# V loads on another queue, whole-batch DMA transposes and a reordered first tile in an attention-plus-MLP kernel

## The chip, the cores and the metric

The kernel runs on one core of one Trainium2 chip. The metric is device time in microseconds (us) for one execution, from the first instruction to the last. A core has several engines that run their own instruction streams side by side: TensorE (PE, with its weight loads listed as PEld), VectorE (DVE), ScalarE (ACT), GpSimd (POOL) and SyncE (SP). SP computes nothing here; it issues DMAs. Sixteen DMA engines move the data, whoever issues the DMA.

## The reference

Eight batches of eight heads, 576 positions of 64 elements, go through causal attention with a window of 64 positions. The heads of a position are laid side by side, which gives x with 4608 rows of 512. A gated MLP with 2048 hidden units follows.

```
scores = scale * np.matmul(q, k.transpose(0, 1, 3, 2))
mask = (rel >= 0) & (rel < window)
scores = np.where(mask, scores, -1000000000.0)
attn = np.exp(scores - max); attn = attn / sum(attn)
x = (attn @ v).transpose(0, 2, 1, 3).reshape(B * S, H * D)
h = x @ w_in
g = h * np.clip(h + 3.0, 0.0, 6.0) / 6.0
out = g @ w_out
```

## The kernel before, in words

**Two kinds of work on one TensorE stream.** The MLP is cut into nine tiles of 512 rows (T = 0 to 8). A tile has a first half, `s1` (16 column blocks of the hidden layer, four matmuls each, into a PSUM bank chosen by `s1_bank`; ACT and DVE make the gate `gT`, lines 538 and 539), and a second half, `s2` (16 steps of four matmuls, line 568, into the banks `o` and `acc`; a finished 128-row block is copied by ACT and stored, line 577). Both halves are generators; after each `yield` other work can be put between. That other work is the attention of a later batch: a tile's 512 rows are less than a batch's 576, so batch b has to be ready a little before tile b starts. There is no scheduler: the order of each engine's instructions is the order in which the Python program emits them (`tc.manual_schedule`), and each engine and each DMA queue runs its own in that order, waiting on semaphores where data is not there.

**What attention of a batch needs.** Heads are taken in four pairs g. Q and K arrive as float32, POOL casts them to bf16 (`qn_all`, `kn_all`), and they must be transposed to Q^T and K^T (`QT`, `KT`). For batches 0 and 1 the PE does that (`main_t`, called by `T_` and `TT`; `rest_t`, called by `RR`, for the last 64 positions). From batch 2 on DMA transposes do it, issued by SP: batch 2 with one for each pair and operand (`transpose_pairs_by_dma`, eight, line 280), the later ones with one for each operand (`transpose_by_dma`, lines 271 to 275). Then `scores` makes the score blocks of a pair in two halves u (line 354), ACT takes the exponential (line 362), `masked` multiplies by the mask on DVE (line 372), `pv` multiplies by V and divides by the sums (`N_`), and the result is transposed into `xT`, the MLP's input: on the PE with an ACT copy (`xt_pe`, `X_`, lines 417 and 422) for batches 0 to 3, by a DMA transpose on SP (`xt_dma`, line 477) for batches 4 to 7.

**Where these calls stand.** For batch 1 they are written out by hand between the steps of tile 0's second half: each `go()` is one step of `s2`. `rest_s`, `rest_n`, `rest_x` finish the last 64 positions of batch 0 there. From tile 1 on `stage_` runs a tile, and `pieces` says after which step of `s1` (p1) or `s2` (p2) a call of the next batch stands. Batch 2 goes through tile 1, batch 3 through tile 2, and so on. Batch 3 has a row of its own in `pieces`, with its first scores after step 13 of tile 2's `s1` and its `X_` calls in tile 2's `s2`. In tiles 1 and 2 the last two x^T transposes of the tile's own batch are put between the first matmuls of the tile.

**The queues.** The POOL queue takes, in this order, the first weights `w_in`, Q and K of batch 1 (heads 0 to 3), the rest of the weights, the tails of batches 0 and 1, and at last tile 0's four held output blocks (line 845). Between these stand POOL's casts. SP's queue takes Q, K, V of batch 0; V of batch 1, held back by `after` until the third block of `w_out` has landed; the 15 loads of batch 2 (Q, K, V, five each); its eight transposes; and then for each tile T the 15 loads of batch T + 2, the tile's output stores, the x^T transposes of batch T + 1, and the two transposes of batch T + 2. A transpose in the queue waits for POOL's casts, a store for ACT's copy, and all behind it wait too:

```
            p2.setdefault(6 if T < 3 else 12, []).append(lambda bt=nxt: bt.transpose_by_dma())
```

so in tiles 1 and 2 of the kernel before, the two whole-operand transposes stand after step 6 of `s2`, behind one store.

Of the kernel before, what the change touches and what calls it, by code (L numbers as in the profile page):

```python
# [24 lines left out]
def kernel(  # L25
# [53 lines left out]
    def load_v(b, vst, h0, h1):  # L79
        out = []  # L80
        for h in range(h0, h1):
            out.append(nc.sync.dma_start(
                out=vst[:, 0 : KB - 1, h, :],
                in_=v[b, h, 0:SM, :].rearrange("(k p) d -> p k d", p=P),
            ))
        return out

    def load_blocks(t, src, b, kbs, tail=0):
        out = []
        for kb in kbs:  # L90
            s0 = kb * P
            ss = min(P, S - s0)
            p0 = tail if ss < P else 0
            out.append(nc.sync.dma_start(  # L94
                out=t[p0 : p0 + ss, kb, :, :],
                in_=src[b, :, s0 : s0 + ss, :].rearrange("h s d -> s h d"),
            ))
        return out
# [22 lines left out]
    def load_v_by_head(b):  # L121
        vst = stage.tile([P, KB, H, D], F32, name="vst", tag="vst")
        ins = load_blocks(vst, v, b, (KB - 1,), SR) + load_v(b, vst, 0, H)
        return vst, ins

    def load_for_dma(b):
        sts, ins = [], []
        for n, src in (("qst", q), ("kst", k), ("vst", v)):
            t = stage.tile([P, KB, H, D], F32, name=n, tag=n)
            ins += load_blocks(t, src, b, range(KB), SR if src is v else 0)  # L130
            sts.append(t)
        return tuple(sts), ins
# [108 lines left out]
    class Batch:  # L241
# [28 lines left out]
        def transpose_by_dma(self):  # L270
            for n, T in ((qn_all, self.QT), (kn_all, self.KT)):
                nc.sync.dma_start_transpose(
                    out=T[:].rearrange("d g (k s) -> d (g k) s", s=P),
                    in_=n[:].rearrange("p g k h d -> p (g k h d)"),
                )

        def transpose_pairs_by_dma(self):
            for g in range(NG):
                for n, T in ((qn_all, self.QT), (kn_all, self.KT)):
                    nc.sync.dma_start_transpose(  # L280
                        out=T[:, g, :].rearrange("d (k s) -> d k s", s=P),
                        in_=n[:, g, :, :, :].rearrange("p k h d -> p (k h d)"),
                    )
# [210 lines left out]
    def s1_bank(fc, T):  # L494
        if T == 0:
            if fc in (6, 7):
                return (ps_o, ps_acc)[fc - 6].tile([P, 512], F32, name=("o", "acc")[fc - 6])[:]
            if fc in (8, 9, 12, 13):
                return ps_st.tile([P, 2, 512], F32, name=f"st{fc % 2}")[:, 0, :]
            return h_bank()[:]  # L500
        if T > 1 and fc < 2:
            return ps_st.tile([P, 2, 512], F32, name=f"st{fc}")[:, 0, :]
# [152 lines left out]
    w_in.append(load_w_in(1536, 2048, 0, NG))  # L655
    w_out = [load_w_out(0, 4)]
# [52 lines left out]
    ld.rest()  # L709
# [14 lines left out]
    bt.cast_qk(st, 1, 0, 4, pcopy)  # L724
    w_out += [load_w_out(4 * i, 4 * i + 4) for i in (1, 2)]
    rst0, rvst0 = load_rest_of_first()
    w_out.append(load_w_out(12, 16))
    vst1, insv = load_v_by_head(1)
    for x in insv:
        after(x, w_out[2], "the weights go first")  # L730
    bt.cast_rest(st, pcopy)
    cast_pairs(bt, st, 4, 4)
    bt0.cast_rest((None, None, rst0), pcopy)
# [4 lines left out]
    run(m)  # L738

    pcopy(out=bt0.V[SR:P, KB - 1, :, 0:D], in_=rvst0[SR:P, :, :])  # L740
    bt.cast_v_end(vst1, pcopy)
    for g in range(NG):
        bt.cast_v(vst1, 2 * g, 2 * g + 2, pcopy)
    st2, _ = load_for_dma(2)

    def st_tr(u):
        t = ps_st.tile([P, 2, 1024], BF16, name=f"st{u}")
        return iter((t[:, 0, :], t[:, 1, :]))

# [13 lines left out]
    S1_(0, 0, 0)  # L763
    S1_(1, 0, 1)
    go(2)
    RR(bt, st_tr(0))
    go()
    S1_(0, 1, 1)
    go()
    S1_(1, 1, 0)  # L770
    TT(bt, 2, st_tr(1))
    go(2)
    TT(bt, 3, st_tr(0))
    go()
    S1_(2, 0, 1)
    go()
    S1_(2, 1, 0)
    go()
    S1_(3, 0, 1)
    go()  # L780
    S1_(3, 1, 0)
    go()
    RR(bt0, st_tr(1))
    go()
    rest_s(bt0, 0)
    go()
    rest_n(bt0, 1)
    go()
    N_(bt, 0, st_pair(0))
    go()  # L790
    N_(bt, 1, oa)
    rest_x(bt0, 0)
    go()
    two = st_tr(1)
    X_(bt, 0, two)
    X_(bt, 1, two)
# [23 lines left out]
    def pieces(bt):  # L820
# [4 lines left out]
        if bt.b == 2:  # L825
            return p1, {
                1: [f(SS, 0)], 2: [f(SS, 1)], 4: [f(N_, 0), f(SS, 2)], 6: [f(X_, 0)], 7: [f(N_, 1), f(SS, 3)],
                9: [f(X_, 1)], 11: [f(N_, 2)], 13: [f(N_, 3)],
            }
        if bt.b == 3:  # L830
            return {13: [f(SS, 0)]}, {
                0: [f(SS, 1)], 3: [f(N_, 0), f(SS, 2)], 5: [f(X_, 0)], 6: [f(N_, 1), f(SS, 3)],
                8: [f(X_, 1)], 9: [f(N_, 2)], 11: [f(X_, 2)], 12: [f(N_, 3)], 14: [f(X_, 3)],
            }
# [8 lines left out]
    bt2.cast_for_dma(st2, (0, 1))  # L843
    for u0, osb in held:
        nc.gpsimd.dma_start(out=out[u0 : u0 + P, :], in_=osb[:])
    bt2.cast_for_dma(st2, (2,))
    bt2.transpose_pairs_by_dma()
    nxt, pend = bt2, None
    for T in range(1, NTB):
# [3 lines left out]
        if b < B:  # L853
# [5 lines left out]
            p2.setdefault(6 if T < 3 else 12, []).append(lambda bt=nxt: bt.transpose_by_dma())  # L859
# [31 lines left out]
```

## Time and profile before

| | us |
|---|---|
| median of 5 runs (lowest to highest) | 315.57 (314.49 to 317.58) |
| the profiled execution | 315.3 |
| its span, first to last instruction | 313.5 |
| PE busy in the span | 299.6 |
| DVE, ACT, POOL busy | 174.3, 177.6, 93.3 |
| start of tile 1, 2, 3, 4 on the PE | 58.1, 92.3, 127.4, 158.9 |
| bytes moved by DMA | 52.80 MB |

The 1.8 us between the span and the execution's time lie outside the instructions. The page lists busy time for each engine, then the span in 40 slices of 7.8 us with the busy share in tenths; its DMA row is the mean busy share of the 16 DMA engines. "a <- b" in a list of waits means that a waited for b. In the chain of waits each row is a start, a duration and what ran; a DMA's row runs from its issue to its landing. In the timeline of SP a row is the time in which SP issued, not the time in which the data moved. "L94" is line 94 of the kernel; `SPq` is SP's queue.

### The profile page before, as it was taken

What the parts mean: (1) busy time and instruction counts of PE and PEld (TensorE: products, weight loads), DVE (VectorE), ACT (ScalarE), POOL (GpSimd) and SP (SyncE); (2) the same over time, 40 slices, a digit from 0 to 9 for tenths busy, and PEclk for the clock granted to TensorE, in tenths of its full rate; (3) what the DMA queues carried; (4) which work ended last, traced back from release to release, by engine and by line L of the source; (5) the groups of instructions that cost most, each with busy time, mean ns of one, the idle gap of its engine ahead of it and who ended that gap; (6) DMA issues with size and microseconds to landing.
All of it is one profiled execution on the core that took longest, in us unless ns stands there. A gap on an engine that the chain in (4) does not pass through costs nothing.

```text
span 313.5 us, 5579 instructions
## 1 busy us (share of the span) xinstructions
PE 299.6 (96%) x2125; PEld 147.8 (47%) x2162; DVE 174.3 (56%) x334; ACT 177.6 (57%) x264; POOL 93.3 (30%) x137
## 2 busy tenths in 40 slices
PE   8898989899999899999999999999999999999995
PEld 3454435544654355445544554455445544444442
DVE  4558545485635765477437753785378627306700
ACT  3857744487627754687158715881588147317611
POOL 5786626363035143305610660155000000000000
PEclk9999999999999999999999999999999999999999
DMA  7999999999799999999999999999900730010011
GB/s 245 201 206 255 242 193 191 213 190 234 165 207 188 268 217 182 205 252 204 216 223 223 203 216 235 216 201 192 246 10 2 127 94 0 33 69 33 0 69 67
DMA packets 147579, 52.80 MB, mean 168 GB/s; under 512 B 136384, under 2 KB 142528, under 8 KB 147552
## 3 DMA queue, kind: packets, MB, share of 16 engines
q1 hardware_dynamic: 141920, 44.18, 69.1%
q0 software_dynamic: 5360, 8.00, 12.9%
q8 instruction: 17, 0.28, 0.4%
q10 hardware_dynamic: 272, 0.26, 0.2%
q14 instruction: 10, 0.08, 0.1%
HBM read 36.70 MB, written 9.44 MB: 147 GB/s over the span
## 4 chain that ended last, share of the span: by engine, by line
PE 73%; DMA 14%; SPq 4%; POOL 2%; ACT 2%; DVE 2%; issue 1%; POOLq 0%
PE o L568 17%; PE acc L568 16%; PE h L531 15%; PE acc L531 5%; PE o L531 5%; PE st L531 5%; DMA wout<-in_moe_w_out_dram 4%; PE st L354 3%; DMA qst<-in_q_dram 3%; DMA kst<-in_k_dram 3%; DMA vst<-in_v_dram 3%; SPq L94 2%; PE h L384 2%; DMA KT<-kn 1%; PE h L389 1%
## 5 line engine op out<-in xcount | busy, mean ns | idle before, releaser
L531 PEld LDWEIGHTS <-win 128*128 128x128 bf16 x576 | 55.1, 98 | 66.0 <-issue 1.7
L568 PEld LDWEIGHTS <-gT 128*128 128x128 bf16 x576 | 52.5, 98 | 57.9 <-issue 1.4
L568 PE MATMUL o<-wout,gT 128*128 128x512 bf16 x261 | 63.8, 380 | 1.5 <-DMA wout<-in_moe_w_out_dram 0.8
L531 PE MATMUL h<-xT,win 128*128 128x512 bf16 x259 | 62.8, 379 | 0.3
L568 PE MATMUL acc<-wout,gT 128*128 128x512 bf16 x261 | 62.3, 379 | 0.6
L362 ACT ACTIVATE pT<-st 128x768 bf16<-128x768 f32 x64 | 48.7, 808 | 14.6 <-PE st L354 14.4
L539 DVE SCALAR_TENSOR_TENSOR gT<-t,st 128x512 bf16<-128x512 bf16 (+1 forms) x26 | 20.7, 809 | 56.7 <-ACT t L538 56.6
L538 ACT ACTIVATE t<-h,half 128x512 bf16<-128x512 f32 x66 | 44.7, 690 | 8.6 <-PE h L531 8.2
L539 DVE SCALAR_TENSOR_TENSOR gT<-t,h 128x512 bf16<-128x512 bf16 x66 | 44.6, 685 | 8.9 <-ACT t L538 8.8
L372 DVE TENSOR_TENSOR pT<-pT,mask 128x1536 bf16<-128x1536 bf16 x28 | 28.2, 1011 | 22.5 <-ACT pT L362 22.5
L258 POOL CAST qn<-qst 128x512 bf16<-128x512 f32 x24 | 16.4, 719 | 71.1 <-DMA qst<-in_q_dram 66.9
L574 ACT COPY osb<-acc 128x512 f32<-128x512 f32 x17 | 10.0, 586 | 42.5 <-PE acc L568 42.5
L531 PE MATMUL st<-xT,win 128*128 128x512 bf16 x125 | 30.4, 379 | 0.7 <-DVE gT L539 0.3
L574 ACT COPY osb<-o 128x512 f32<-128x512 f32 x17 | 10.0, 588 | 29.9 <-PE o L568 29.9
L406 DVE TENSOR_TENSOR opg<-h,rec 128x320 bf16<-128x320 f32 x50 | 24.6, 492 | 1.7
L531 PE MATMUL o<-xT,win 128*128 128x512 bf16 x89 | 23.4, 379 | 0.5 <-DVE gT L539 0.3
L538 ACT ACTIVATE t<-st,half 128x512 bf16<-128x512 f32 (+1 forms) x26 | 20.1, 785 | 6.4 <-PE st L531 6.1
L531 PE MATMUL acc<-xT,win 128*128 128x512 bf16 x91 | 23.6, 379 | 0.1
L248 POOL CAST V<-vst 128x512 bf16<-128x512 f32 (+1 forms) x14 | 16.5, 1179 | 16.6 <-DMA vst<-in_v_dram 13.7
L384 PEld LDWEIGHTS <-pT 128*128 128x128 bf16 x256 | 17.5, 97 | 7.7 <-PE h L417 0.5
L258 POOL CAST kn<-kst 128x512 bf16<-128x512 f32 x24 | 14.4, 639 | 18.7 <-DMA kst<-in_k_dram 15.0
L354 PE MATMUL st<-QT,KT 64*128 64x192 bf16 (+2 forms) x312 | 17.5, 230 | 1.7 <-DMA KT<-kn 0.9
(111 smaller groups left out, 282.3 us busy)
## 6 DMA issues: line engine op xcount, KB each, us to landing
out_dram<-osb SPq DMA_DIRECT2D x32, 256.0 KB, 2.5
qst<-in_q_dram SPq DMA_DIRECT2D x28, 256.0 KB, 4.8
kst<-in_k_dram SPq DMA_DIRECT2D x27, 256.0 KB, 5.5
vst<-in_v_dram SPq DMA_DIRECT2D x24, 256.0 KB, 5.4
vst<-in_v_dram SPq DMA_DIRECT2D x23, 128.0 KB, 4.1
win<-in_moe_w_in_dram POOLq DMA_DIRECT2D x4, 512.0 KB, 7.4
wout<-in_moe_w_out_dram POOLq DMA_DIRECT2D x4, 512.0 KB, 13.3
qst<-in_q_dram POOLq DMA_DIRECT2D x2, 512.0 KB, 11.7
```

The source lines that it names most:

```text
L248: copy(out=self.V[:, 0 : KB - 1, h0:h1, 0:D], in_=vst[:, 0 : KB - 1, h0:h1, :])
L258: pcopy(out=n[:, g, 0 : KB - 1, :, :].rearrange("p k h d -> p k (h d)"), in_=s[:, 0 : KB - 1, 2 * g : 2 * g + 2, :].rearrange("p k h d -> ...
L354: nc.tensor.matmul(st[:, h, o0 : o0 + n], lhsT=bt.KT[h * D : (h + 1) * D, g, k0 : k0 + P], rhs=bt.QT[h * D : (h + 1) * D, g, q0 : q0 + n], ...
L362: nc.scalar.activation(out=pT[:, :, 2 * u : 2 * u + 2, 0:QW], in_=st[:, :, 0:w].rearrange("p h (k w) -> p h k w", k=2), func=EXP, scale=scale,
L372: nc.vector.tensor_tensor(out=pT[:, :, :, 0:QW], in0=pT[:, :, :, 0:QW], in1=mask[:].rearrange("p (h k) w -> p h k w", h=2), op=MULT,)
L384: nc.tensor.matmul(ob, lhsT=pT[:, h, qb, 0:P], rhs=V[:, qb, 2 * g + h, :], start=True, stop=(qb == 0),)
L406: nc.vector.tensor_tensor(out=opgs[bt.b, g][:, 0:nb, h, :], in0=ov[:, :, 0:D], in1=rec[:, 0:nb].unsqueeze(2).to_broadcast([P, nb, D]), op= ...
L531: nc.tensor.matmul(hT, lhsT=win16[:, g, fc * P : (fc + 1) * P], rhs=xT[:, g, t0 : t0 + TB], start=(g == 0), stop=(g == NG - 1),)
L538: nc.scalar.activation(out=t1[:], in_=hT, func=RELU, bias=half[:], scale=1.0 / 6.0)
L539: nc.vector.scalar_tensor_tensor(out=out, in0=t1[:], scalar=1.0, in1=hT, op0=MIN, op1=MULT,)
L568: nc.tensor.matmul(accs[ts], lhsT=gT[:, fc, ts * P : (ts + 1) * P], rhs=wout16[:, fc, :], start=(fc == 0), stop=(fc == NFC - 1),)
L574: acopy(out=osb[:], in_=accs[ts])
```

## The change

V of batch 1 is issued on POOL's queue, behind the last weights, and the first load of batch 2 waits for the seventh of these nine loads. The tail of batch 1 is loaded ahead of the first block of `w_out` and cast earlier. In tile 0 the two score halves of a pair stand together, the tail transposes of batch 1 stand before the last step of `s1`, two copies for the tail of batch 0 go from POOL to DVE, and two `xt_pe` transposes are issued before either is copied. Batch 2's Q^T and K^T come from one DMA transpose each, with V's five loads between them in SP's queue. Batch 3 loses its own row in `pieces`: its scores start after step 10 of tile 2's `s1`, and its x^T comes from four DMA transposes. Tiles 1 and 2 use other PSUM banks in `s1`; in tile 1 the transposes of batch 3 stand after step 8, in tile 2 those of batch 4 after step 12.

```
--- before.py
+++ after.py
@@ -76,22 +76,22 @@
 
 
 
-    def load_v(b, vst, h0, h1):
+    def load_v(b, vst, h0, h1, eng=None):
         out = []
         for h in range(h0, h1):
-            out.append(nc.sync.dma_start(
+            out.append((eng or nc.sync).dma_start(
                 out=vst[:, 0 : KB - 1, h, :],
                 in_=v[b, h, 0:SM, :].rearrange("(k p) d -> p k d", p=P),
             ))
         return out
 
-    def load_blocks(t, src, b, kbs, tail=0):
+    def load_blocks(t, src, b, kbs, tail=0, eng=None):
         out = []
         for kb in kbs:
             s0 = kb * P
             ss = min(P, S - s0)
             p0 = tail if ss < P else 0
-            out.append(nc.sync.dma_start(
+            out.append((eng or nc.sync).dma_start(
                 out=t[p0 : p0 + ss, kb, :, :],
                 in_=src[b, :, s0 : s0 + ss, :].rearrange("h s d -> s h d"),
             ))
@@ -120,12 +120,13 @@
 
     def load_v_by_head(b):
         vst = stage.tile([P, KB, H, D], F32, name="vst", tag="vst")
-        ins = load_blocks(vst, v, b, (KB - 1,), SR) + load_v(b, vst, 0, H)
+        ins = load_blocks(vst, v, b, (KB - 1,), SR, nc.gpsimd) + load_v(b, vst, 0, H, nc.gpsimd)
         return vst, ins
 
-    def load_for_dma(b):
+    def load_for_dma(b, which=(0, 1, 2)):
         sts, ins = [], []
-        for n, src in (("qst", q), ("kst", k), ("vst", v)):
+        for i in which:
+            n, src = (("qst", q), ("kst", k), ("vst", v))[i]
             t = stage.tile([P, KB, H, D], F32, name=n, tag=n)
             ins += load_blocks(t, src, b, range(KB), SR if src is v else 0)
             sts.append(t)
@@ -267,20 +268,13 @@
                 self.cast_v(st[2], 0, H, pcopy)
                 self.cast_v_end(st[2], pcopy)
 
-        def transpose_by_dma(self):
-            for n, T in ((qn_all, self.QT), (kn_all, self.KT)):
+        def transpose_by_dma(self, which=(0, 1)):
+            for i in which:
+                n, T = ((qn_all, self.QT), (kn_all, self.KT))[i]
                 nc.sync.dma_start_transpose(
                     out=T[:].rearrange("d g (k s) -> d (g k) s", s=P),
                     in_=n[:].rearrange("p g k h d -> p (g k h d)"),
                 )
-
-        def transpose_pairs_by_dma(self):
-            for g in range(NG):
-                for n, T in ((qn_all, self.QT), (kn_all, self.KT)):
-                    nc.sync.dma_start_transpose(
-                        out=T[:, g, :].rearrange("d (k s) -> d k s", s=P),
-                        in_=n[:, g, :, :, :].rearrange("p k h d -> p (k h d)"),
-                    )
 
         def cast_qk(self, st, i, h0, heads, copy):
             n = (qn_all, kn_all)[i][:].rearrange("p g k h d -> p (g k h d)")[:, 0 : R * H * D]
@@ -498,6 +492,12 @@
             if fc in (8, 9, 12, 13):
                 return ps_st.tile([P, 2, 512], F32, name=f"st{fc % 2}")[:, 0, :]
             return h_bank()[:]
+        if T < 3 and fc in (6, 7):
+            return (ps_o, ps_acc)[fc - 6].tile([P, 512], F32, name=("o", "acc")[fc - 6])[:]
+        if T == 2:
+            if fc % 4 < 2:
+                return h_bank()[:]
+            return (ps_o, ps_acc)[fc % 2].tile([P, 512], F32, name=("o", "acc")[fc % 2])[:]
         if T > 1 and fc < 2:
             return ps_st.tile([P, 2, 512], F32, name=f"st{fc}")[:, 0, :]
         if T > 1:
@@ -653,6 +653,7 @@
     ld.main(0, 0, 4)
     ld.main(1, 0, 4)
     w_in.append(load_w_in(1536, 2048, 0, NG))
+    ld.rest()
     w_out = [load_w_out(0, 4)]
     pcopy(out=bt.V[0:SR, KB - 1, :, 0:D], in_=bt.V[SR:P, KB - 2, :, 0:D])
 
@@ -706,7 +707,6 @@
     run(m, 1)
 
 
-    ld.rest()
     ld.main(0, 4, 8)
     ld.main(1, 4, 8)
     bt0, st1 = bt, ld.tiles
@@ -722,30 +722,30 @@
     bt, st = Batch(1), st1
     bt.cast_qk(st, 0, 0, 4, pcopy)
     bt.cast_qk(st, 1, 0, 4, pcopy)
+    bt.cast_rest(st, pcopy)
     w_out += [load_w_out(4 * i, 4 * i + 4) for i in (1, 2)]
     rst0, rvst0 = load_rest_of_first()
+    cast_pairs(bt, st, 4, 4)
     w_out.append(load_w_out(12, 16))
     vst1, insv = load_v_by_head(1)
-    for x in insv:
-        after(x, w_out[2], "the weights go first")
-    bt.cast_rest(st, pcopy)
-    cast_pairs(bt, st, 4, 4)
-    bt0.cast_rest((None, None, rst0), pcopy)
     run(m, 11)
     TT(bt, 0, oa_tr)
     run(m, 2)
     TT(bt, 1, oa_tr)
+
+    def st_tr(u):
+        t = ps_st.tile([P, 2, 1024], BF16, name=f"st{u}")
+        return iter((t[:, 0, :], t[:, 1, :]))
+
+    run(m, 2)
+    RR(bt, st_tr(0))
     run(m)
 
-    pcopy(out=bt0.V[SR:P, KB - 1, :, 0:D], in_=rvst0[SR:P, :, :])
     bt.cast_v_end(vst1, pcopy)
     for g in range(NG):
         bt.cast_v(vst1, 2 * g, 2 * g + 2, pcopy)
-    st2, _ = load_for_dma(2)
-
-    def st_tr(u):
-        t = ps_st.tile([P, 2, 1024], BF16, name=f"st{u}")
-        return iter((t[:, 0, :], t[:, 1, :]))
+    st2, ins2 = load_for_dma(2, (0, 1))
+    after(ins2[0], insv[6], "the values go first")
 
     def st_pair(u):
         t = ps_st.tile([P, 2, 512], F32, name=f"st{u}")
@@ -760,40 +760,38 @@
     def go(n=1):
         run(m, n)
 
-    S1_(0, 0, 0)
-    S1_(1, 0, 1)
+    def SS1_(g):
+        S1_(g, 0, 0)
+        S1_(g, 1, 1)
+
+    SS1_(0)
     go(2)
-    RR(bt, st_tr(0))
+    SS1_(1)
+    go(2)
+    TT(bt, 2, st_tr(0))
     go()
-    S1_(0, 1, 1)
+    TT(bt, 3, st_tr(1))
+    go(2)
+    SS1_(2)
+    go(2)
+    SS1_(3)
+    go(2)
+    bt0.cast_rest((None, None, rst0), vcopy)
+    RR(bt0, st_tr(0))
+    go(2)
+    rest_s(bt0, 1)
     go()
-    S1_(1, 1, 0)
-    TT(bt, 2, st_tr(1))
-    go(2)
-    TT(bt, 3, st_tr(0))
-    go()
-    S1_(2, 0, 1)
-    go()
-    S1_(2, 1, 0)
-    go()
-    S1_(3, 0, 1)
-    go()
-    S1_(3, 1, 0)
-    go()
-    RR(bt0, st_tr(1))
-    go()
-    rest_s(bt0, 0)
+    vcopy(out=bt0.V[SR:P, KB - 1, :, 0:D], in_=rvst0[SR:P, :, :])
+    N_(bt, 0, st_pair(0))
     go()
     rest_n(bt0, 1)
+    N_(bt, 1, oa)
     go()
-    N_(bt, 0, st_pair(0))
-    go()
-    N_(bt, 1, oa)
     rest_x(bt0, 0)
-    go()
     two = st_tr(1)
-    X_(bt, 0, two)
-    X_(bt, 1, two)
+    two = [xt_pe(bt, g, next(two)) for g in range(2)]
+    two[0]()
+    two[1]()
     N_(bt, 2, oa)
     N_(bt, 3)
 
@@ -824,13 +822,8 @@
         p1, p2 = {}, {}
         if bt.b == 2:
             return p1, {
-                1: [f(SS, 0)], 2: [f(SS, 1)], 4: [f(N_, 0), f(SS, 2)], 6: [f(X_, 0)], 7: [f(N_, 1), f(SS, 3)],
-                9: [f(X_, 1)], 11: [f(N_, 2)], 13: [f(N_, 3)],
-            }
-        if bt.b == 3:
-            return {13: [f(SS, 0)]}, {
-                0: [f(SS, 1)], 3: [f(N_, 0), f(SS, 2)], 5: [f(X_, 0)], 6: [f(N_, 1), f(SS, 3)],
-                8: [f(X_, 1)], 9: [f(N_, 2)], 11: [f(X_, 2)], 12: [f(N_, 3)], 14: [f(X_, 3)],
+                2: [f(SS, 0)], 4: [f(SS, 1)], 6: [f(N_, 0), f(SS, 2)], 8: [f(N_, 1), f(SS, 3)],
+                9: [f(X_, 0)], 11: [f(N_, 2)], 12: [f(X_, 1)], 14: [f(N_, 3)],
             }
         p1 = {10: [f(SS, 0)], 13: [f(SS, 1)]}
         p2 = {
@@ -840,11 +833,14 @@
         return p1, p2
 
     bt2 = Batch(2)
-    bt2.cast_for_dma(st2, (0, 1))
+    bt2.cast_for_dma(st2, (0,))
+    bt2.transpose_by_dma((0,))
+    (vst2,), _ = load_for_dma(2, (2,))
+    bt2.cast_for_dma(st2, (1,))
+    bt2.transpose_by_dma((1,))
     for u0, osb in held:
         nc.gpsimd.dma_start(out=out[u0 : u0 + P, :], in_=osb[:])
-    bt2.cast_for_dma(st2, (2,))
-    bt2.transpose_pairs_by_dma()
+    bt2.cast_for_dma((None, None, vst2), (2,))
     nxt, pend = bt2, None
     for T in range(1, NTB):
         p1, p2 = pieces(nxt)
@@ -856,7 +852,7 @@
             p1.setdefault(12 if T == 1 else 6, []).append(
                 lambda bt=nxt, sts=sts: bt.cast_for_dma(sts)
             )
-            p2.setdefault(6 if T < 3 else 12, []).append(lambda bt=nxt: bt.transpose_by_dma())
+            p2.setdefault(8 if T == 1 else 12, []).append(lambda bt=nxt: bt.transpose_by_dma())
         stage_(T, None, p1, p2)
```

## The prediction

> **What bounds the kernel now.** I read the page's busy rows first, then the waits of the PE, the chain of waits through tile 2, and SP's timeline.
>
> ```profile
> PE 299.6 (96%) x2125; PEld 147.8 (47%) x2162; DVE 174.3 (56%) x334; ACT 177.6 (57%) x264; POOL 93.3 (30%) x137
> ...
> DMA  7999999999799999999999999999900730010011
> ```
>
> The PE looks like the only bound. But the DMA engines are as full until slice 28 (about 227 us), so two resources run side by side. Where they meet is in the chain, here between 90 and 128 us:
>
> ```profile
> 94.95 5.24 DMA vst<-in_v_dram
> ...
> 102.21 4.23 DMA KT<-kn
> 106.44 0.05 issue
> 106.48 0.51 PE st L354 x10
> ...
> 127.39 0.81 PE st L531 x3
> ```
>
> K^T of batch 3 lands at 106.44 and the PE's scores start 0.04 us later. The PE's waits between 58 and 128 us say how much that cost:
>
> ```profile
> PE st L354 <- DMA KT<-kn: 0.9, 1, 0.9
> ...
> PE o L531 <- DVE gT L539: 0.3, 1, 0.3
> PE st L531 <- DVE gT L539: 0.3, 1, 0.3
> ```
>
> Only 0.9 us: the order of the work matches the data's arrival closely. From 127.4 on (tile 3) each tile takes 31.8 us with no such wait, so every us in the start of tile 3 is a us in the end. I reduce the question to that start: 127.39 before. The last view is SP's timeline after batch 2's loads:
>
> ```profile
> 67.39 1.30 SPq L280 DMA_TRANSPOSE QT<-qn  x1
> ...
> 78.20 1.27 SPq L280 DMA_TRANSPOSE KT<-kn  x1
> 79.52 5.76 SPq L94 DMA_DIRECT2D qst<-in_q_dram  x5
> ```
>
> Eight transposes hold SP for 12.1 us. In the windows of 76 to 80 and 80 to 84 us the DMA share is 0.58 and 0.66, against 1.1 around them: the DMA stream has a hole here, because SP issues too slowly.
>
> **Edits that end under a wait.** Score halves together and the paired x^T copies can remove the PE's wait of 0.9 us on ACT (L417 at 56.89) and small ones of 0.16 to 0.24 us beside it; tile 1 then starts at about 57.4 instead of 58.1. The new banks in `s1` can remove the two 0.3 us waits on `gT`. The two copies moved to DVE take 0.6 and 1.4 us on POOL; DVE is busy for 5.2 of 10 us there, so I cost them at nothing (without that cover 1 us, ahead of batch 0's tail). The earlier tail of batch 1 puts 256 KB, some 1.7 us by landings, ahead of the first `w_out` block: it lands at 34.1 instead of 32.5, and its first matmul is at 34.2. POOL now waits for that tail until about 31.4, and behind it stand the next two `w_out` issues, 32.0 instead of 28.5; these have 11.5 us from issue to landing because the queue is backed up, so their landing at 40.05 should hold (otherwise up to 1 us in tile 0). All this gains 1 to 1.5 us before batch 2's scores, and is lost if these wait for data.
>
> **V of batch 1 on POOL's queue.** Nine issues at 0.7 us (the rows of POOL's other loads) are 6.3 us on POOL, from about 39 to 48, where POOL was idle 6 us anyway; behind them stand the V casts, from about 48.6 (48.5 before). V's landings were 48.5 to 53.1 at 0.54 us each. In POOL's queue a 128 KB load landed 0.6 to 0.9 us after the last. Best: V ends at 51.7, as 44 to 50 us moved only 140 to 174 GB/s; worst: 0.75 us each, 54.5. A rule speaks against any gain: the Trainium skill, "DMA: Bandwidth & Descriptors", section "Issuing engines are not separate DMA queues", says that all queues share the same DMA engines and only the sequencer's issue time is saved. By the best row V is 1.4 us early, by the rule 0. I take the rule, because `w_out`'s last block (47.76) is ahead of V on either queue. Then the new wait: batch 2's first load waits for the sixth head's landing (about 51.5), while issue to landing took 3.8 us at 50.49. It lands at 55.1 rather than 54.30: **+0.8 us** (−1.4 to +2.5) on the stream.
>
> **Two transposes for eight.** Before, from batch 2's last V (70.75) to batch 3's first Q block (84.36) went 13.6 us. The work in it: four output blocks, 3.9; eight transposes of a pair, equal to 2 x 2.4 (Q^T and K^T of batch 3 landed 2.5 and 2.4 after what was ahead); a first block, 1.2; latency 0.5. Sum 10.4, so the hole is worth **−3.2 us**. The stream reaches batch 4's last V at 127.23 + 0.8 − 3.2 = 124.8.
>
> But for batch 2 itself K^T is now the last thing, complete for all pairs at once, behind V. Stream: batch 1's V at 53.1, +0.8, batch 2's loads 17.7, Q^T 2.4, four stores 3.9, K^T 2.4 = 80.3; what the stores fit into thin spots I take as 1 us: **79.2**. Before, pair 0 was complete at 75.2, and pairs came as needed. The PE reaches these scores one step later than before: 57.4 + 17.15 + 0.86 − 0.3 = 75.1. So it waits **4.1 us** (2 to 5), and the gains of tile 0 go into that wait.
>
> Here a second rule of the skill speaks against the change: "TensorE: Matmul & The Clock Gate", section "Why this matters for your kernels": an idle gap of over some 3 us puts the PE back to half clock, and the page gives a window of about 3.4 us until it is released. The longest PE gap inside this trace is 1.3 us and the PEclk row is 9 throughout. By the row the wait costs itself; by the rule up to half of 3.4 = 1.7 us more (an estimate from that page). I take none, since 4.1 is near the edge, and keep 1.7 for the range.
>
> Tile 2 then starts at 79.2 + (92.33 − 75.28) − 0.86 = 95.4.
>
> **x^T of batch 3 by DMA.** It frees the PE of 20 transposes, four groups of 0.28 = 1.1 us in tile 2, and ACT of four copies of 0.55. Tile 2 took 35.06; less 1.1, less the 0.9 wait on K^T, less 0.3 and small gaps: 32.5. (Batch 3's K^T: one more store stands ahead of it, so 106.44 − 2.4 + 1.0 = 105.0; the scores moved three steps up are reached at 95.4 + 10.7 = 106.1. No wait.) So the PE would be ready for tile 3 at 95.4 + 32.5 = 127.9. But the four transposes stand in SP's queue behind batch 4's 15 loads, among the stores. The nearest row is tile 3, where batch 4 does this already:
>
> ```profile
> 149.23 2.30 SPq L94 DMA_DIRECT2D vst<-in_v_dram  x2
> 151.62 0.57 SPq L577 DMA_DIRECT2D out_dram<-osb  x1
> 152.29 2.67 SPq L477 DMA_TRANSPOSE xT<-opg  x2
> 155.05 0.54 SPq L577 DMA_DIRECT2D out_dram<-osb  x1
> 155.69 2.55 SPq L477 DMA_TRANSPOSE xT<-opg  x2
> ```
>
> Its last x^T landed at 159.61, 4.9 us after the last V (4.5 and 5.5 in the next tiles), just as tile 4 needed it (start 158.94, fourth matmul 0.65 later). In tile 2 the loads run later against the PE. Last x^T: 124.8 + 5.0 = 129.8; less 0.65 gives tile 3 at **129.2**, later than the PE's 127.9. This decides. The moved transposes of batch 4 (after step 12) follow at about 136 to 137, wanted at 129.2 + 9.4 = 138.6: free. Later tiles: the stream between K^T and x^T shrinks by two stores, and the tile stays 31.8.
>
> **Sum.** 129.2 − 127.4 = +1.8 us. On the profiled execution 315.3 + 1.8 = 317.1; that execution is 0.3 below the median, so the median gives 315.6 + 1.8 = **317.4**.
>
> **Rivals.**
> A, the above: the data sets the start of tile 3, 128.4 to 130.4, so 316.6 to 318.6. Chance 0.47. For it: tile 3's row. Against: three landings are estimated.
> B, not slower: one stream without holes. Fed earlier, SP also loses its stalls of 2.1 to 2.6 us in the loads of batches 3 and 4; at the spacing of 1.2 and 0.7 us a batch takes 16.5 instead of 17.6, with V 0.4 to 1 us earlier. Last V of batch 4 at 120.4, tile 3 at 124.8: 313.0. It decides from a last V before 121.5 and a K^T of batch 2 before 77. If the PE alone set it, 57.4 + 32.6 + 32.5 = 122.5, so 310.7 is the floor. Against: these stalls come in every tile, in 63.8 as in 115.7. Chance 0.17.
> C, even: the hole is worth 4.5 and both arrivals come near 127.5: 315.7. Chance 0.15.
> D, clearly slower: V at 0.75 us each (+1.7) or the half clock (+1.7), tile 3 at 132.3: 320.5. Chance 0.21.
> That the change doesn't do what it says has one form: x^T leaves the PE, and the PE waits for it instead; that is A.
>
> **Numbers.** A measurement here tells about 0.5% from no change, 314.0 to 317.15. B gives faster 0.17; C and the lower part of A (0.13) give same 0.28; the rest is slower, 0.55. The range 313.0 to 321.0 leaves out B's and D's ends, 0.08 each. A's own range is 316.6 to 318.6.
>
> **What would show it.** Right: a PE wait of 2 to 5 us on K^T at the first scores of tile 1, near 79; SP without the 12 us of transposes; the last V of batch 4 near 125; a PE wait at tile 3's first matmuls on a DMA into `xT`; tiles of 31.8 after it. Wrong: tile 3 before 127, no `xT` wait, or the first load of batch 2 landing well before 54. Fewer PE transposes and shorter waits in tile 0 prove nothing, as they are under the waits.

## The result, and the profile after

The changed kernel is slower by 0.63% (ratio 1.0063, interval 1.0043 to 1.0084), which is 2.0 us on the 315.3 us of the kernel before in the same runs; the prediction had +1.8. The medians of all executions are 318.46 us (27) against 315.32 (48), which is 3.1 us. The ratio leaves out executions more than 1.5% above the fastest of their kernel; of the changed kernel that is a third, the profiled one (321.1 us, span 319.4) among them, and all of these had a mean granted clock of 0.995 or less, which experiment 3 below traces to the change itself.

Here are the page's rows of the changed kernel: the engines' busy time, the granted clock and the DMA engines, in 40 slices of 8.0 us.

```profile
PE 300.4 (94%) x2106; PEld 147.8 (46%) x2142; DVE 176.7 (55%) x336; ACT 173.8 (54%) x260; POOL 101.2 (32%) x144
...
PEclk9999999998799999999999999999999999999999
DMA  7999996999999999899989999998920440020011
```

Two slices of the PEclk row, the tenth and eleventh, fall to 8 and 7. The DMA row is as full as before: data and PE still run side by side. The waits of the PE between 58 and 133 us, the stretch of tiles 1 and 2:

```profile
PE st L348 <- DMA KT<-kn: 4.1, 1, 4.1
PE o L568 <- DVE gT L539: 1.9, 1, 1.9
PE h L531 <- DVE gT L539: 0.6, 2, 0.3
```

The wait on K^T is 4.1 us, as forecast, but it is batch 2's. There is no wait on `xT`. In its place a wait of 1.9 us on a gate stands before the second half of tile 2. The chain of waits through both tiles shows the same; ACT's exponentials (L356) and DVE's mask (L366) of batch 3's scores stand in it ahead of that gate:

```profile
71.44 8.17 DMA KT<-kn
79.66 0.82 PE st L348 x7
...
112.25 1.51 ACT pT L356 x2
113.78 1.39 DVE pT L366
115.17 0.61 DVE gT L539
115.82 1.02 PE o L568 x4
...
132.83 1.73 PE st L531 x8
```

SP's timeline, here from 62 to 80 us, has lost the eight transposes, and its first load of batch 3 stands at 77.53 instead of 79.52:

```profile
62.69 3.89 SPq L274 DMA_TRANSPOSE QT<-qn  x1
66.88 4.40 SPq L94 DMA_DIRECT2D vst<-in_v_dram  x5
71.44 6.05 SPq L274 DMA_TRANSPOSE KT<-kn  x1
77.53 2.53 SPq L94 DMA_DIRECT2D qst<-in_q_dram  x3
```

The x^T transposes of batch 3 went out on SP from 122.71 on:

```profile
122.71 2.61 SPq L471 DMA_TRANSPOSE xT<-opg  x2
126.09 0.37 SPq L577 DMA_DIRECT2D out_dram<-osb  x1
126.55 2.60 SPq L471 DMA_TRANSPOSE xT<-opg  x2
```

The last was issued at 127.96 and landed at 130.59. Tile 3's first matmul is at 132.67.

### The profile page after: what moved, and what is told of

It reads as the page before. It is cut to its first block, busy times and chain, and to the rows that moved or that the text cites. A ratio compares the mean times of both kernels' runs of the same rounds, so it can differ in the third digit from the quotient of the medians.

```text
span 319.4 us, 5535 instructions
## 1 busy us (share of the span) xinstructions
PE 300.4 (94%) x2106; PEld 147.8 (46%) x2142; DVE 176.7 (55%) x336; ACT 173.8 (54%) x260; POOL 101.2 (32%) x144
## 4 chain that ended last, share of the span: by engine, by line
PE 69%; DMA 14%; SPq 7%; POOL 3%; ACT 2%; DVE 2%; issue 2%; POOLq 0%
PE acc L568 17%; PE o L568 17%; PE h L531 14%; PE o L531 5%; PE acc L531 5%; SPq L94 5%; PE st L531 4%; DMA rst<-in_k_dram 4%; PE st L348 3%; DMA vst<-in_v_dram 3%; DMA wout<-in_moe_w_out_dram 3%; DMA KT<-kn 3%; PE h L378 2%; DMA qst<-in_q_dram 1%; PE h L383 1%
## 5 line engine op out<-in xcount | busy, mean ns | idle before, releaser
L568 PEld LDWEIGHTS <-gT 128*128 128x128 bf16 x576 | 53.3, 98 | 61.2 <-issue 3.9
L568 PE MATMUL o<-wout,gT 128*128 128x512 bf16 x264 | 65.5, 383 | 2.4 <-DVE gT L539 1.9
L356 ACT ACTIVATE pT<-st 128x768 bf16<-128x768 f32 x64 | 48.5, 808 | 23.7 <-PE st L348 23.6
L539 DVE SCALAR_TENSOR_TENSOR gT<-t,st 128x512 bf16<-128x512 bf16 (+1 forms) x24 | 19.3, 820 | 59.3 <-ACT t L538 59.3
L366 DVE TENSOR_TENSOR pT<-pT,mask 128x1536 bf16<-128x1536 bf16 x28 | 30.4, 1086 | 28.9 <-ACT pT L356 28.9
L531 PE MATMUL st<-xT,win 128*128 128x512 bf16 x116 | 28.5, 379 | 0.6 <-DMA win<-in_moe_w_in_dram 0.4
L531 PE MATMUL o<-xT,win 128*128 128x512 bf16 x95 | 24.6, 379 | 0.1
L531 PE MATMUL acc<-xT,win 128*128 128x512 bf16 x95 | 24.6, 379 | 0.1
L259 POOL CAST kn<-kst 128x512 bf16<-128x512 f32 x24 | 16.0, 707 | 18.5 <-DMA kst<-in_k_dram 11.7
L538 ACT ACTIVATE t<-st,half 128x512 bf16<-128x512 f32 (+1 forms) x24 | 18.7, 793 | 5.8 <-PE st L531 5.5
```

The lines of the kernel that those rows point to most:

```text
L259: pcopy(out=n[:, g, 0 : KB - 1, :, :].rearrange("p k h d -> p k (h d)"), in_=s[:, 0 : KB - 1, 2 * g : 2 * g + 2, :].rearrange("p k h d -> ...
L356: nc.scalar.activation(out=pT[:, :, 2 * u : 2 * u + 2, 0:QW], in_=st[:, :, 0:w].rearrange("p h (k w) -> p h k w", k=2), func=EXP, scale=scale,
L366: nc.vector.tensor_tensor(out=pT[:, :, :, 0:QW], in0=pT[:, :, :, 0:QW], in1=mask[:].rearrange("p (h k) w -> p h k w", h=2), op=MULT,)
L531: nc.tensor.matmul(hT, lhsT=win16[:, g, fc * P : (fc + 1) * P], rhs=xT[:, g, t0 : t0 + TB], start=(g == 0), stop=(g == NG - 1),)
L538: nc.scalar.activation(out=t1[:], in_=hT, func=RELU, bias=half[:], scale=1.0 / 6.0)
L539: nc.vector.scalar_tensor_tensor(out=out, in0=t1[:], scalar=1.0, in1=hT, op0=MIN, op1=MULT,)
```

## Experiments

After the result I held two theories of where the time goes. Theory 1: the PE's own order decides the start of tile 3; the wait on K^T, a clock that falls after it, and the wait on a PSUM bank add up. Theory 2, my prediction: x^T of batch 3, at the end of the data's stream, decides it. "Stream" below is the row of DMAs from the first weights to batch 4's V. Its position shifts by up to 2.6 us between profiles of kernels whose code is the same up to there (with tile 0's new order the second `w_out` block landed anywhere from 37.5 to 40.1), so I compare lengths of tiles and distances in the stream, and times by the ratio against the kernel before on the same chip. The lists of waits are the PE's, between 58 and 130 us where nothing else is said, cut below their longest waits. Starts of tiles on the PE, and lengths, in us:

| kernel | tile 1 | tile 2 | tile 3 | length 1 | length 2 | ratio (interval) |
|---|---|---|---|---|---|---|
| before | 58.13 | 92.33 | 127.39 | 34.2 | 35.1 | 1 |
| changed | 57.80 | 97.78 | 132.67 | 40.0 | 34.9 | 1.0063 (1.0043 to 1.0084) |
| old banks | 58.65 | 96.21 | 129.01 | 37.6 | 32.8 | 1.0049 (1.0025 to 1.0074) |
| x^T on PE | 59.03 | 98.82 | 137.17 | 39.8 | 38.4 | 1.0163 (1.0114 to 1.0212) |
| fill | 58.26 | 94.34 | 128.82 | 36.1 | 34.5 | 1.0098 (1.0063 to 1.0134) |
| K^T first | 57.11 | 92.58 | 127.03 | 35.5 | 34.5 | 1.0106 (1.0055 to 1.0156) |
| pairs | 58.82 | 92.31 | 135.03 | 33.5 | 42.7 | 1.0219 (1.0184 to 1.0255) |
| V on SP | 57.91 | 92.00 | 126.45 | 34.1 | 34.5 | 1.0048 (1.0027 to 1.0070) |
| batch 3's row | 58.15 | 92.28 | 127.85 | 34.1 | 35.6 | 1.0130 (1.0079 to 1.0182) |
| pairs, old banks | 58.82 | 92.31 | 130.08 | 33.5 | 37.8 | 1.0158 (1.0118 to 1.0199) |
| V on SP, old banks | 57.24 | 91.79 | 124.74 | 34.6 | 33.0 | 1.0031 (1.0006 to 1.0056) |
| and V of batch 4 late | 58.77 | 92.59 | 125.39 | 33.8 | 32.8 | 1.0105 (1.0053 to 1.0157) |
| and K^T first | 57.82 | 93.02 | 126.02 | 35.2 | 33.0 | 1.0168 (1.0121 to 1.0215) |
| tile 0 alone | 58.25 | 92.38 | 126.29 | 34.1 | 33.9 | 1.0014 (0.9991 to 1.0037) |

**1. Old banks in tile 2.**

```diff
-        if T < 3 and fc in (6, 7):
+        if T < 2 and fc in (6, 7):
...
-        if T == 2:
-            if fc % 4 < 2:
-                return h_bank()[:]
-            return (ps_o, ps_acc)[fc % 2].tile([P, 512], F32, name=("o", "acc")[fc % 2])[:]
```

> The changed kernel with one part undone: tile 2's first half uses the PSUM banks of the kernel before, so that its last two blocks stand in h and not in o and acc. The profile of the changed kernel shows the first matmul of tile 2's second half waiting 1.9 us for the gate of a block that still stands in bank o. Theory 1 (PE order decides the start of tile 3: the wait on K^T, the clock after it, and this bank wait add up): the 1.9 us wait goes, a wait of 0.3 us on gT comes back, and the time falls by 1 to 1.6 us against the changed kernel, to a ratio of about 1.002 to 1.005 against the kernel before. Theory 2 (the landing of batch 3's x^T decides, as I predicted): tile 3 starts with a wait on a DMA into xT instead, and the time falls by less than 0.5 us.

The waits between 58 and 130 us in this kernel:

```profile
PE st L348 <- DMA KT<-kn: 2.4, 1, 2.4
PE o L527 <- DVE gT L535: 0.3, 1, 0.3
PE h L527 <- DVE gT L535: 0.3, 1, 0.3
```

The wait of 1.9 us is gone and tile 2 is 2.1 us shorter. With the changed banks blocks 14 and 15 of tile 2 stand in `o` and `acc`, where the second half's first sums go, so the PE waits until ACT and DVE have emptied the bank; these two engines have just been given batch 3's second scores. This is theory 1's third part, as far as the trace goes. What it is worth in time is not clear of noise: the ratio fell by 0.0014 only, within both intervals (by 0.0026 between the medians of all executions), which is less than 2.1 us. The same edit lowered it in the two other pairs of runs too (9 against 6 by 0.0017, 8 against 5 by 0.0061). In this profile the last x^T landed at 128.68 and tile 3 started at 129.01, so part of the gain would soon have met theory 2.

**2. x^T of batch 3 on the PE, at the steps of the changed kernel.**

```diff
+        xt = X_ if bt.b == 3 else xt_dma
...
-            0: [f(SS, 2)], 1: [f(N_, 0)], 2: [f(SS, 3)], 3: [f(N_, 1), f(xt_dma, 0)],
+            0: [f(SS, 2)], 1: [f(N_, 0)], 2: [f(SS, 3)], 3: [f(N_, 1), f(xt, 0)],
```

(and so for the other three)

> The changed kernel with batch 3's x^T made on the PE again, at the steps where the changed kernel issues the DMA transposes. Theory 1 (PE order decides): tile 2 has 1.1 us more PE work and no wait goes, so the time rises by about 1.1 us, to a ratio of about 1.010. Theory 2 (x^T's landing decides): the time falls by 0.5 to 1.3 us, to a ratio of about 1.003. Either way the wait on K^T of batch 2 stays at 2 to 5 us.

The ratio rose by 0.010, three times what theory 1 gave. Tile 2 is 3.5 us longer: 1.1 us of transposes, and new waits on `opg` of 2.8 us in all, since the transpose now stands right behind the product whose division DVE has not finished. So it is no pure undo of that part; run 7 comes nearer.

**3. Matmuls that fill the wait.**

```diff
+        def fill():
+            t = h_bank()
+            for _ in range(12):
+                nc.tensor.matmul(
+                    t[:], lhsT=xT[:, 0, 0:P], rhs=xT[:, 0, 0:TB], start=True, stop=True,
+                )
...
-                2: [f(SS, 0)], 4: [f(SS, 1)], 6: [f(N_, 0), f(SS, 2)], 8: [f(N_, 1), f(SS, 3)],
+                2: [fill, f(SS, 0)], 4: [f(SS, 1)], 6: [f(N_, 0), f(SS, 2)], 8: [f(N_, 1), f(SS, 3)],
```

> The changed kernel with twelve matmuls of 512 columns added before batch 2's first scores, which nobody reads; they fill 2.6 us of the wait on K^T, so that the PE's idle stretch is at most 2 us. Theory 1a (the wait of 4 us also costs clock: the PEclk row of the changed kernel falls to 0.5 for 80 to 84 us after it): the granted clock stays at 1.00, tile 2 starts about 2.4 us earlier in the profile and the median of all runs falls by 1 to 2 us. Theory 1b (the clock is chance and has nothing to do with this wait): the clock falls as often as before, and the time stays or rises by up to 1 us where the wait was shorter than the fill.

Windows by engine, from 76 us on; the columns are the stretch, its length, busy time (instructions) of PE, PEld, DVE, ACT, POOL, then granted clock, DMA share, GB/s. First the changed kernel, then run 1, then this one:

```profile
76.00:80.00 4.00, 0.34 (x6) 0.32 (x8) 0.00 (x0) 0.00 (x0) 2.82 (x3) 0.72 1.16 200
80.00:84.00 4.00, 3.78 (x17) 1.35 (x16) 0.96 (x1) 2.10 (x3) 0.30 (x1) 0.50 1.26 227
84.00:88.00 4.00, 4.00 (x48) 2.52 (x48) 1.94 (x4) 2.12 (x3) 2.55 (x4) 0.92 1.32 201
```

```profile
76.00:80.00 4.00, 1.63 (x14) 0.64 (x13) 0.00 (x0) 0.86 (x2) 3.12 (x3) 0.89 1.12 240
80.00:84.00 4.00, 3.78 (x21) 1.52 (x21) 0.96 (x1) 2.19 (x4) 0.00 (x0) 0.69 1.33 204
```

```profile
76.00:80.00 4.00, 3.84 (x27) 1.85 (x26) 0.00 (x0) 1.09 (x2) 1.78 (x3) 1.00 1.18 231
80.00:84.00 4.00, 4.00 (x49) 2.25 (x47) 2.20 (x4) 2.47 (x5) 1.06 (x1) 1.00 1.35 193
```

The first shows half clock for a whole window after a wait of 4.1 us, the second a shorter spell after 2.4 us, the third none. If the clock is either whole or half, the missing shares make 6.9 us of half clock in the first and 3.4 in the second (an estimate from these rows). From batch 2's first scores to tile 2 the first took 18.1 us and the second 17.5; seven profiles that kept a clock of 1.00 there (runs 3 and 5 to 10) all took 15.8 with the same instructions. So the clock cost 2.3 us after the wait of 4.1, and 1.6 after that of 2.4. (Of the 6.9 us some 1.9 fell into the wait itself, by the first row and its 0.34 us of work.)

Half clock for 3.4 us lowers the mean clock of an execution to about 0.995, so I count executions at that or less. In the changed kernel these are 16 of 28 with the profiled one, median 319.2 us, and the other 12 have a median of 317.1; with this fill they are 0 of 7, in the kernel before 7 of the 75 of these sessions. Sorted by the longest wait of the PE from 58 to 165 us in the profile of each run, they are 1 of 14 with 0.3 us (run 12), 15 of 60 with 1.0 to 1.7 (runs 3, 4, 6, 7, 9, 10, 11), 11 of 22 with 2.4 (run 1), and 33 of 47 with 3.0 to 5.5 (runs 2, 5, 8 and the changed kernel). So the clock falls because the PE is idle there: theory 1a on the clock holds. The time is a miss: the ratio of the medians of all executions is 1.0090 against 1.0100, not 1 to 2 us better. In this profile K^T landed at 76.95, 1.1 us after the fill began, so that of its 2.7 us 1.6 were added to the time, and the wait without the fill would have been about 1.1 us; the count over all executions, not this one profile, speaks for the fill.

**4. K^T of batch 2 ahead of its V.**

```diff
     bt2.transpose_by_dma((0,))
-    (vst2,), _ = load_for_dma(2, (2,))
     bt2.cast_for_dma(st2, (1,))
     bt2.transpose_by_dma((1,))
+    (vst2,), _ = load_for_dma(2, (2,))
```

> The changed kernel with K^T of batch 2 ahead of V's five loads in SP's queue, instead of behind them. Theory 1 (the wait on K^T, 4.1 us in the profile, is a matter of queue order): K^T lands at 72 to 75, the wait at the first scores of tile 1 goes, the clock stays at 1.00, and V of batch 2 lands near 79.6 and is cast by 83, which is when its first use comes. Tile 2 starts at 92 to 93 instead of 97.8. If the PE's order decides the rest, the time falls by 3 to 5 us, to a ratio of about 0.992 to 0.997. Theory 2 (the data's stream as a whole decides, and x^T of batch 3 lands near 130 in any case): tile 3 starts with a wait on xT at 129 to 130, and the time falls by 1 us or less, to a ratio of 1.002 or more.

```profile
PE h L389 <- POOL V L254: 1.6, 1, 1.6
PE o L568 <- DVE gT L539: 1.5, 1, 1.5
PE h L531 <- DVE gT L539: 0.6, 2, 0.3
```

K^T landed at 72.80 and nobody waited for it. But V's last load landed at 78.14 and its cast to bf16 ended at 81.4, so the PE waited for V instead, for 1.6 us, and the clock fell in 3 of 6 executions (not in the profiled one). The ratio is no better than the changed kernel's. The wait is passed along the queue, not removed.

**5. Eight transposes of a pair for batch 2 again.**

```diff
-    bt2.cast_for_dma(st2, (0,))
-    bt2.transpose_by_dma((0,))
     (vst2,), _ = load_for_dma(2, (2,))
-    bt2.cast_for_dma(st2, (1,))
-    bt2.transpose_by_dma((1,))
+    bt2.cast_for_dma(st2, (0, 1))
...
     bt2.cast_for_dma((None, None, vst2), (2,))
+    bt2.transpose_pairs_by_dma()
```

(with the function `transpose_pairs_by_dma` of the kernel before)

> The changed kernel with batch 2's Q^T and K^T in eight transposes of a pair again, behind V's loads, as in the kernel before; all else stays. Theory 1 (the wait on K^T and the clock after it are most of the change's loss): the first pair is complete near 76, the waits on K^T at tile 1's scores are 1 us or less, the clock stays at 1.00, tile 2 starts at 92 to 93 instead of 97.8, and the ratio falls to about 0.998 to 1.003. Theory 2 (the stream of data is what counts): the hole in it comes back, batch 4's loads and batch 3's x^T are about 3 us later, near 133, and tile 3 waits for x^T; the ratio is then 1.010 or more.

The waits between 58 and 136 us:

```profile
PE st L356 <- DMA KT<-kn: 5.5, 1, 5.5
PE o L576 <- DVE gT L547: 1.6, 1, 1.6
PE h L539 <- DVE gT L547: 0.6, 2, 0.3
```

Tile 1 has no wait on K^T any more. The wait is in tile 2, on batch 3's K^T, which lands at 108.43 (105.30 in the changed kernel) while the scores, moved up to step 10, stand ready near 103; the clock falls after it, in 6 of 6 executions. Theory 2 is right about the stream and wrong about the place: x^T isn't what is late, K^T of the next batch is. The last V of batch 4 lands 73.3 us after batch 2's first load here and 70.4 in the changed kernel: the two transposes are worth some 3 us of stream, and the moved-up scores spend them. (Over all profiles this stretch is 71.4 to 73.3 us with eight transposes and 68.3 to 71.1 with two, where batch 4's V was not moved.)

**6. V of batch 1 on SP's queue.**

```diff
-        ins = load_blocks(vst, v, b, (KB - 1,), SR, nc.gpsimd) + load_v(b, vst, 0, H, nc.gpsimd)
+        ins = load_blocks(vst, v, b, (KB - 1,), SR) + load_v(b, vst, 0, H)
...
+    for x in insv:
+        after(x, w_out[2], "the weights go first")
...
-    after(ins2[0], insv[6], "the values go first")
```

> The changed kernel with V of batch 1 on SP's queue again, released as in the kernel before by the third block of w_out. My prediction puts 0.8 us on the move to POOL's queue, because batch 2's first load waits for a landing of V there. If that is right: batch 2's first load lands near 54.3 instead of 55.1, K^T of batch 2 at 78.8 instead of 79.6, and the time falls by about 0.8 us. If the queue of V doesn't matter: K^T lands at the same time as in the changed kernel within 0.3 us, and the ratio stays at about 1.006.

```profile
PE o L568 <- DVE gT L539: 1.5, 1, 1.5
PE h L531 <- DVE gT L539: 0.6, 2, 0.3
PE st L348 <- DMA KT<-kn: 0.5, 1, 0.5
```

From V's last landing to batch 2's first it took 1.1 us here, 1.2 in the kernel before and 1.1 to 1.5 in runs 9 to 12, all with V on SP's queue; it took 2.4 in the changed kernel and 1.8 to 2.4 in the profiles of runs 1 to 5, 7 and 8, all with V on POOL's queue: about 0.9 us between the means, the 0.8 of my sum. The rest of the shorter wait in this profile (0.5 us on K^T against 4.1) is not this edit's: the stream was early before it (`w_out`'s last block landed at 45.59 against 46.75), and K^T came 23.6 us after batch 2's first load instead of 24.5. The medians of all executions have a ratio of 1.0053 against 1.0100, which is 1.5 us, and the clock is at 0.995 or less in 2 of 15. So a shift of about 1 us goes with a clock that mostly stays whole. The intervals of the ratios (1.0027 to 1.0070 and 1.0043 to 1.0084) overlap.

**7. Batch 3's own row again.**

```diff
+        if bt.b == 3:
+            return {13: [f(SS, 0)]}, {
+                0: [f(SS, 1)], 3: [f(N_, 0), f(SS, 2)], 5: [f(X_, 0)], 6: [f(N_, 1), f(SS, 3)],
+                8: [f(X_, 1)], 9: [f(N_, 2)], 11: [f(X_, 2)], 12: [f(N_, 3)], 14: [f(X_, 3)],
+            }
```

> The changed kernel with batch 3's own row in the table of pieces again, as in the kernel before: its first scores after step 13 of tile 2's first half, x^T on the PE at the steps of the kernel before. Prediction's sum: x^T by DMA saves 1.1 us of PE work, and the wait on x^T takes it all back. If that holds, undoing it costs nothing or gains: ratio 1.000 to 1.006. If the PE's order decides, undoing it costs 1.1 us and more: tile 2 takes at least 1.1 us longer than in the changed kernel (34.9), and the ratio is 1.009 or more.

Tile 2 is 0.7 us longer than in the changed kernel and 1.1 longer than in the runs 3, 4 and 6 with the same banks (34.5); the ratio is 1.0130. So x^T by DMA saves its 1.1 us of PE work, with the reserve that this run also puts batch 3's first scores three steps back. My sum had the 1.1 given back in full; it isn't.

**8. Pairs and old banks together.** The edits of 5 and 1.

> The changed kernel with two parts undone: eight transposes of a pair for batch 2, and the PSUM banks of the kernel before in tile 2. Theory 1 (PE order and waits alone): tile 1 takes 34.2 us as before, tile 2 takes 32.8 us as with the old banks, so tile 3 starts near 124.5 and the time falls to a ratio of about 0.991. Theory 2 (the landing of x^T is the next limit): with the hole in the stream x^T of batch 3 lands near 132 and tile 3 starts with a wait on a DMA into xT of several us; the ratio is 1.003 or more. If it lies between, both bind in turn.

```profile
PE st L356 <- DMA KT<-kn: 3.0, 1, 3.0
```

K^T of batch 3 was waited for by 3.0 us, the clock fell in 6 of 6, tile 3 began at 130.08 with the last x^T at 130.50: neither theory alone. The ratio, 1.0158, falls in what theory 2 allowed, by a K^T wait that it didn't name.

**9. V on SP and old banks.** The edits of 6 and 1.

> The changed kernel with two parts undone: V of batch 1 on SP's queue, and the old PSUM banks in tile 2. With V on SP alone the profile had tile 3 at 126.5 with a wait of 1.5 us on bank o in tile 2, and batch 3's last x^T at 126.0. If waits on the PE add up (theory 1): the bank wait goes, tile 3 starts at 124.8, ratio 0.999 to 1.001. If x^T is the next limit (theory 2, my prediction's, now that the PE is early enough): tile 3's matmuls wait for x^T for about 0.5 to 1 us near 125, ratio 1.001 to 1.003.

```profile
PE st L348 <- DMA KT<-kn: 1.0, 1, 1.0
PE st L527 <- DMA xT<-opg: 0.5, 1, 0.5
PE h L527 <- DVE gT L535: 0.3, 1, 0.3
PE o L527 <- DVE gT L535: 0.3, 1, 0.3
```

Here the wait that I had forecast appears, as theory 2 said: tile 3 begins at 124.74 and stops for x^T, whose last part lands at 125.96; tile 3 is 32.4 us long instead of 31.8. With two of the losses undone the PE is early enough that x^T is the next limit. It has the lowest ratio of the runs with the change's data order, and is still not faster than the kernel before.

**10. V of batch 4 behind x^T.**

```diff
-            sts, _ = load_for_dma(b)
+            late = T == 2
+            sts, _ = load_for_dma(b, (0, 1) if late else (0, 1, 2))
...
+            if late:
+                def v_late(bt=nxt):
+                    (t,), _ = load_for_dma(bt.b, (2,))
+                    bt.cast_for_dma((None, None, t), (2,))
+
+                p2.setdefault(11, []).append(v_late)
```

> As the run before, and V of batch 4 is loaded behind batch 3's x^T in SP's queue (after step 11 of tile 2's second half), since it is first used in tile 3's second half. Theory 2 (x^T's landing limits tile 3 once the PE is early): x^T lands 3 us earlier or more, near 122, no wait on x^T stays, and the time falls by 0.5 to 1.5 us against the run before, to a ratio of 0.996 to 0.999. Theory 1 (only the PE's own waits count): no difference within 0.3 us, or a loss where V of batch 4 comes late for tile 3.

The waits from tile 1 to tile 4, 58 to 165 us:

```profile
PE st L348 <- DMA KT<-kn: 1.5, 2, 1.3
PE st L527 <- DMA xT<-opg: 0.8, 1, 0.8
```

x^T of batch 3 landed at 123.23 and tile 3 didn't wait for it. But now batch 4's K^T (136.26) and x^T (160.08) were waited for, and tiles 3 and 4 took 33.1 us each. Expected was a gain; the ratio is 1.0105. Moving one load back in a full stream moves the wait one tile on.

**11. K^T first and later products with V, on top of 10.** In tile 1 the products stand after steps 7 and 9.

> As the run with V of batch 4 late, and in tile 1 K^T of batch 2 goes ahead of V of batch 2 in SP's queue, with the products with V one or two steps later (7 and 9 instead of 6 and 8). With K^T first alone, the wait moved from K^T to V's last block (1.6 us). Theory 1 (both waits are queue order): neither K^T nor V is waited for by more than 0.3 us, the clock stays at 1.00 in all runs, tile 1 takes 33.5 us instead of 34.2, and the ratio is 0.993 to 0.997, below both kernels. Theory 2 (the stream as a whole): a new wait of 1 us or more on K^T of batch 3 or x^T takes its place, ratio 0.998 or more.

The waits from tile 1 to tile 4, 58 to 165 us:

```profile
PE st L348 <- DMA KT<-kn: 1.7, 1, 1.7
PE st L527 <- DMA xT<-opg: 1.2, 2, 0.8
PE h L411 <- DVE opg L400: 0.8, 1, 0.8
PE h L389 <- POOL V L254: 0.6, 1, 0.6
```

Theory 1 missed: tile 1 took 35.2 us, with waits on V and on `opg`. Theory 2 had the ratio right, but not the place: the waits on K^T and x^T are batch 4's, in tiles 3 and 4, and not batch 3's. The ratio is 1.0168, the highest but one.

**12. Tile 0's new order alone, on the kernel before.** The changed kernel with the edits of 5, 6 and 7, the old banks in all tiles, and the old steps of batches 2 to 4.

> The kernel before with the new order of tile 0 alone: score halves together, earlier tail of batch 1, two copies on DVE, paired x^T copies; V on SP, eight transposes of a pair, batch 3's own row, and old banks stay. Prediction: tile 1 starts 0.7 us earlier on the PE, and the gain goes into the waits on K^T behind it because the data doesn't come earlier; ratio 0.998 to 1.001. The rival, that tile 0 costs time (the profile of the changed kernel has waits of 1.0, 0.9, 0.6 and 0.5 us there that the kernel before has not): tile 1 starts no earlier than 58.1, ratio 1.000 to 1.004.

The waits between 30 and 58 us, first in the kernel before, then here:

```profile
PE st L417 <- ACT xT L422: 0.9, 1, 0.9
PE o L568 <- DMA wout<-in_moe_w_out_dram: 0.8, 1, 0.8
```

```profile
PE st L301 <- DVE rn L296: 1.4, 1, 1.4
PE st L356 <- ACT KT L310: 1.0, 1, 1.0
PE st L419 <- DVE opg L408: 0.6, 1, 0.6
PE st L466 <- DVE opr L458: 0.6, 1, 0.6
```

The wait of 0.9 us that I meant to see go is gone, and so is the one on the weights, but four others came: for the tail's cast, now behind the masks on DVE; for the tail's K^T, which the second half of the first pair's scores now needs at once; and for two divisions. Tile 1 starts at 58.25. The ratio, 1.0014, can't be told from no change.

## Why the prediction was right, and where it was wrong

The direction and the size were right: +1.8 us forecast, +2.0 measured by the ratio (+3.1 between the medians of all executions), within A's range. Its data side, point by point, in the profile of the changed kernel: batch 2's first load 55.1 forecast, 55.12 measured; its K^T 79.2, 79.61; the wait on it 4.1, 4.1; batch 3's K^T 105.0, 105.30, with no wait as forecast; batch 4's last V 124.8, 125.50; the last x^T 129.8, 130.59. The first of these agrees in part by chance: my own terms, 51.5 and 3.8, make 55.3, and the trace has 51.72 and an issue at 51.87 that took 3.25 to land. The 3.2 us for the hole in the stream is confirmed by run 5 (some 3 us), the 0.8 for V's queue by run 6 (about 0.9), the 1.1 for x^T by run 7.

One step failed, the last: "129.2, later than the PE's 127.9. This decides." x^T didn't decide, since the PE came to tile 3 only at 132.67, after x^T's last landing at 130.59. Two terms of the PE's side were wrong.

- I wrote that the new banks in `s1` can remove two waits of 0.3 us. Two such waits stayed, now on `h`, and in tile 2 the banks added a wait of 1.9 us (1.5 to 1.8 in other runs). I had looked at the waits that the kernel before shows in tile 2's first half and not at who needs `o` and `acc` next. Run 1 shows it: without these banks the wait is gone. This is the true rival to my x^T wait: a loss of the same size at almost the same place.
- I took no price for the clock, with 1.7 us kept for the range. From batch 2's first scores to tile 2 the profiled execution took 18.1 us where I had 16.2 and where profiles at whole clock took 15.8: the price is 2.3 us, more than the 1.7 that I had worked out from the clock-gate rule of the Trainium skill's page "TensorE: Matmul & The Clock Gate", section "Why this matters for your kernels", and the window of 3.4 us that the page gives. The half clock lasted about twice those 3.4 us, though part of it fell into the wait. The rule's "over some 3 us" was generous: in run 1 a wait of 2.4 us was enough to bring the clock to 0.69 for a window. More than half of the executions pay it.

In the executions with the clock above 0.995 the median is 317.1 us, 1.8 above the kernel before and close to my 317.4. None of these was profiled; in the profile of run 6, at whole clock and with the same banks, tile 3 starts at 126.45 after a bank wait of 1.5 us, and the last x^T has landed at 125.97. So the bank wait stands where I had the wait on x^T, and the number is right partly by luck, through a loss that I did not name. Run 9 shows that mine was the next in line: take the bank wait and 1 us of stream away, and x^T is waited for.

Rival B (a stream without holes lets the PE run ahead) failed: SP's long issues stayed, and the stream between batch 2's first load and batch 4's last V was 68.3 to 71.1 us in all runs with two transposes (runs 10 and 11, which move batch 4's V, aside). C needed a hole of 4.5 us; the stream got shorter by 2.5 (72.9 to 70.4). D's half clock happened, in A's company, and D's sum was wrong: the 1.7 us belong to the PE's 127.9, which makes 129.6, hardly later than x^T's 129.2, and not 132.3. Tile 0's gain was smaller than my 0.7 us (0.3, and none in run 12), and no effect on the end can be told in run 12, as I wrote.

The change moves nearly everything and gains little, because its main gain, some 3 us of stream, is used at once: K^T for all pairs of batch 2 comes at the end of its queue instead of pair by pair, batch 3's scores are three steps earlier, and x^T is put on the stream. What stays open is how the loss divides between the wait on K^T, the bank and x^T in time, since the intervals of the single undos overlap with the changed kernel's, and a version that beats the kernel before. Runs 4, 10 and 11 tried orders of the queue, and each found the next thing in the queue waited for.

## What to carry to other kernels

When the PE and the data's stream are both full, price an edit by the next wait in the queue, not by the wait that it removes; and for a large transfer that replaces pieces, ask when the first piece was needed. A change of PSUM banks has to be checked against the next user of the bank in the next phase. An idle stretch of the PE of the length of those seen here (2.4 us and more) should be charged for the clock as well: 1.6 us for the one of 2.4, 2.3 for that of 4.1.

## What the runs showed of the hardware that I had not expected

A wait of 2.4 us, not only of 4, lowers the granted clock: 0.89 and 0.69 in the two windows around it, and 0.50 after 4.1 us. The half clock came in stretches of about 3.4 us (run 1) and 6.9 (the changed kernel), so the longer wait brought about twice the stretch. Executions of one kernel fall in two groups by it, with medians of 317.1 and 319.2 us, so its spread is wider than that of the kernel before (314.4 to 321.2 against 313.2 to 317.8). The position of the whole stream shifts by up to 2.6 us at the second `w_out` block between profiles whose code is the same up to there; I did not find out why.
